# Attention normalisation moved from the output tiles to the queries, value sums folded into the output weights, in a hand-set order

## The chip, the cores and the metric

The kernel runs on one core of one Trainium2 chip. The metric is the device time of one launch in microseconds (us). Single runs of one kernel mostly agree within 0.3%; the 2% that counts as a clear difference is 11.5 us here. In profile lines, PE is TensorE (matmul), DVE is VectorE, ACT is ScalarE, SP is SyncE; "SPq" is the queue from which SyncE issues transfers.

## The reference

A layer with linear attention is followed by a token-mixing MLP.

```python
h  = x + A(layernorm(x))                   # S = 2048 tokens, D = 1024, 32 heads of 32
h2 = h + B(layernorm(h))                   # B mixes tokens: S -> 3584 -> S

def A(x):                                  # cut
    q, k, v = split(x @ wqkv)
    phi = lambda t: where(t > 0, t + 1, exp(t)) + 1e-6
    pq, pk = phi(q), phi(k)
    kv = einsum("bhsd,bhse->bhde", pk, v); z = einsum("bhsd->bhd", pk)
    num = einsum("bhqd,bhde->bhqe", pq, kv)
    den = einsum("bhqd,bhd->bhq", pq, z)[..., None] + 1e-6
    return merge_heads(num / den) @ wo
```

Per head, the output row is `(pq @ kv / den) @ wo`. The reciprocal of `den` is one number per token and head, so it may be applied to `pq` instead; and `kv @ wo` does not depend on the token, so it can be computed once. That algebra is the change.

## The kernel before

The MLP's matmuls are Strassen-like: seven products instead of eight, and in the groups called quads the first and fifth product are split once more into 256-wide matmuls. PSUM is the memory that TensorE adds into; to evacuate a tile is to copy it out of there, to seed it is to copy the residual in first. The stretch that matters starts when keys and values are summed. What remains are 22 units of the query projection (eight 128x512 matmuls each), then 16 output tiles of 128 tokens (sixteen matmuls each), then the first mixer product. Cut:

```python
a3w = actx.enter_context(tc.tile_pool(name="a3w", bufs=3))       # h_bf: evacuated output tiles
xrpool = actx.enter_context(tc.tile_pool(name="xrpool", bufs=XRL + 1))   # residual tiles, 4 buffers

def attn_num_den(i):                          # one tile of 128 tokens
    for j in range(ND):                       # 8 matmuls of 132 columns: 128 numerators, 4 denominators
        b, sl = divmod(j, JPB)
        nc.tensor.matmul(nd_ps[:, b, sl * NCOL:(sl + 1) * NCOL],
                         lhsT=pqT[:, j, i * P:(i + 1) * P], rhs=ndrhs[:, j, :], start=True, stop=True)
    # ... ScalarE: reciprocal as exp(-ln(den)); VectorE: three scalings from PSUM into o_sb
    return o_sb

def attn_transpose(i, o_sb):                  # by DMA, back into the place of the queries
    nc.sync.dma_start_transpose(out=pqT[:, :, i * P:(i + 1) * P], in_=o_sb[:])

def out_proj(i):
    xr = xrs.pop(i)
    h_bf = a3w.tile([P, D], BF16, name="h_bf")
    for dc in range(NDC):
        ap_ = acc_tile()                      # one of five PSUM accumulators, in turn
        nc.scalar.copy(ap_[:, 0:CW], xr[:, dc * CW:(dc + 1) * CW])      # seed with the residual
        # ... eight matmuls pqT x wo_sb on top of the seed
        nc.scalar.copy(h_bf[:, dc * CW:(dc + 1) * CW], ap_[:, 0:CW])
        nc.vector.bn_stats(st[:, dc, :], ap_[:, 0:CW])
    # ... mean, variance, scale
    nc.sync.dma_start(h_dram[i][:], h_bf[:])  # needed again for the last addition

for i in range(NS):
    if i % 2 == 0 and i // 2 < TPC:
        attn(NS - TPC + i // 2)
    if i + XRL < NS:
        load_xr(i + XRL)                      # one residual tile ahead per output tile
    out_proj(i)
    if i >= 2:
        normalize_h(i - 2)
```

A scheduler may reorder what is not pinned. In the timelines ScalarE and SyncE's transfer queue work through their instructions in the order of the built program.

Of the kernel before, what the change touches and what calls it, by code (L numbers as in the profile page):

```python
# [1 line left out]

# [19 lines left out]
XRL = 3  # L22
ACT_SET_LN_EXP = 6
# [4 lines left out]
def kernel(  # L28
# [28 lines left out]
    NCOL = P + HB  # L57
    JPB = BANK // NCOL
    NNB = (ND + JPB - 1) // JPB
# [40 lines left out]
    for q in range(HB):  # L100
        nc.vector.memset(maskbd[q * DH:(q + 1) * DH, q * DH:(q + 1) * DH], 1.0)
        nc.vector.memset(m4[q * DH:(q + 1) * DH, q:q + 1], 1.0)
# [5 lines left out]
    nc.vector.memset(eps_den[:], DEN_EPS)  # L108
# [27 lines left out]
    def load_w1(u, half):  # L136
        if half == 0:
            w1_tiles[u] = w_tile(wpool, WLEN)[:, 0:NS * CW].rearrange("p (k f) -> p k f", f=CW)
        k = slice(half * NSP, (half + 1) * NSP)
        nc.sync.dma_start(  # L140
            w1_tiles[u][:, k, :],
            B_w1[:, u * CW:(u + 1) * CW].rearrange("(k p) f -> p k f", p=P)[:, k, :],
        )
# [8 lines left out]
    def combine(e, o, t2, t3, t4):  # L152
        lo, hi = slice(0, CW), slice(CW, 2 * CW)
        sub = ALU.subtract
        nc.vector.tensor_tensor(t3, o[:, hi], e[:, hi], sub)
        nc.vector.tensor_tensor(e[:, hi], e[:, hi], e[:, lo], sub)
        nc.vector.tensor_tensor(t2, o[:, hi], e[:, hi], sub)
        if t4 is not None:
            nc.vector.tensor_tensor(t4, o[:, lo], t2, sub)
# [29 lines left out]
    def inner_moving(M, nk, pool, name):  # L189
# [4 lines left out]
        def sums():  # L194
            for o, a, b in ((t3, b22, b12), (b12, b12, b11), (t2, b22, b12), (t4, b21, t2)):
                nc.vector.tensor_tensor(o, a, b, ALU.subtract)
# [3 lines left out]
    class Held:  # L200
        on = False

        def __init__(self, engine):
            self.engine = engine

        def __getattr__(self, name):
            op = getattr(self.engine, name)
            return (lambda *a, **kw: pin(op(*a, **kw))) if Held.on else op  # L208

    dve, pe = Held(nc.vector), Held(nc.tensor)  # L210

# [55 lines left out]
    class Product7:  # L267
# [61 lines left out]
        def p6(self, ks=None):  # L329
            self.mm(6, self.B, False, ks)  # L330
            if self.whole(ks):
                self.C = psy.tile([P, BANK], F32, tag="y", name="psC1")
                nc.scalar.copy(self.C[:], self.B[:])  # L333
# [18 lines left out]
        def p4(self, ks=None):  # L352
            for a, b, ps in self.parts:
                self.mm(4, ps, False, ks, cols=slice(a, b))
                if self.whole(ks):
                    self.evac(1, 0, ps, a, b)
            if self.whole(ks):
                self.done()

    class Mixer1(Product7):  # L360
# [11 lines left out]
        def evac_shared(self, fh, ps):  # L372
            t = pools["t"].tile([P, BANK], F32, tag=f"t{fh}", name="t1")
            nc.vector.tensor_tensor(t[:], ps[:], self.e[:], ALU.add)
            self.evac(fh, 1, t)

        def done(self):
            e = gE[:, self.p, :]
            nc.vector.tensor_tensor(e[:, CW:D], e[:, CW:D], e[:, 0:CW], ALU.subtract)
# [39 lines left out]
    class Quad:  # L419
        def __init__(self, sts, mov1, mov5):  # L420
            self.sts = sts
            self.mov1, self.mov5 = mov1, mov5

# [29 lines left out]
        def interleave(self, n, fs):  # L453
            steps = [(f, k) for f in fs for k in range(self.sts[0].nk)]
            t = len(steps)
            cuts = [0, (5 * t + 8) // 16, (9 * t + 8) // 16, (12 * t + 8) // 16, t]

            def fill(q):
                part = steps[cuts[q]:cuts[q + 1]]
                for f in fs:  # L460
                    ks = [k for g, k in part if g is f]
                    if ks:
                        f(ks)

            for f in (n.i1, 0, n.i6, n.i2, 1, n.i5, n.i7, 2, n.i3, 3, n.i4):
                fill(f) if isinstance(f, int) else f()

# [46 lines left out]

        def run(self, pend, nxt, on_p4=nop, before_p7=nop, on_p7=nop, cut=None):
            interleave = self.interleave
            if self.mov1 is not None:
                for st in self.sts:
                    st.begin()
                interleave(self.in1, [st.p4 for st in pend])  # L520
# [9 lines left out]
            interleave(self.in5, [st.p6 for st in self.sts])  # L530
            pre = nxt.pre if nxt is not None else (lambda m: None)
# [8 lines left out]
            pre(7)  # L540
            for st in self.sts:
                st.p3()
            pre(3)
# [14 lines left out]
    def run_pair(st, pend, nxt, after1=nop, after5=nop, on_p4=nop, before_p7=nop, on_p7=nop):  # L558
        st.p1()
        after1()  # L560
        if not pend:
            h = st.nk // 2
            st.p5(list(range(st.nk - 1)))
            st.p2(list(range(h)))
            st.p5([st.nk - 1])
        else:
            for q in pend:
                q.p4()
            on_p4()
            st.p5()  # L570
        after5()
        nxt.pre(5)
        st.p6()
        nxt.pre(6)
        st.p2(None if pend else list(range(h, st.nk)))
        before_p7()
        st.p7()
        on_p7()
        nxt.pre(7)
        st.p3()  # L580
        nxt.pre(3)
        return [st]

    with ExitStack() as actx:
        a3s = actx.enter_context(tc.tile_pool(name="a3s", bufs=4))
        a3w = actx.enter_context(tc.tile_pool(name="a3w", bufs=3))
        a3o = actx.enter_context(tc.tile_pool(name="a3o", bufs=3))
# [7 lines left out]
        ndrhs = pqpool.tile([P, ND, NCOL], BF16)  # L595
# [10 lines left out]
        with ExitStack() as a1:  # L606
# [476 lines left out]
            for n in range(3):  # L1083
                q_fill()
            for b in range(NKB):
                j0, n = b * KPB, min(KPB, ND - b * KPB)
                nc.vector.tensor_tensor(
                    ndrhs[:, j0:j0 + n, 0:P],
# [5 lines left out]
                    ndrhs[:, j0:j0 + n, P:NCOL],  # L1094
# [6 lines left out]
        warmctx.close()  # L1101
        wpool = sactx.enter_context(tc.tile_pool(name="wpool", bufs=2, side="right"))
# [4 lines left out]

        a3p = actx.enter_context(ExitStack())
        ndp = a3p.enter_context(tc.tile_pool(name="ndp", bufs=1, space=PSUM))
        nd_ps = ndp.tile([P, NNB, BANK], F32, name="nd_ps")  # L1110
        nc.vector.memset(nd_ps[:], 0.0)

        with ExitStack() as a3:

            def attn_num_den(i):
                for j in range(ND):
                    b, sl = divmod(j, JPB)
                    nc.tensor.matmul(
                        nd_ps[:, b, sl * NCOL:(sl + 1) * NCOL],
                        lhsT=pqT[:, j, i * P:(i + 1) * P],  # L1120
                        rhs=ndrhs[:, j, :],
                        start=True,
                        stop=True,
                    )
                dn = a3s.tile([P, NNB * JPB * HB], F32, name="dn")
                nc.scalar.activation(
                    dn[:].rearrange("p (b s c) -> p b s c", b=NNB, c=HB),
                    nd_ps[:, :, 0:JPB * NCOL].rearrange("p b (s c) -> p b s c", c=NCOL)[:, :, :, P:NCOL],
                    ACT.Ln,
                    bias=eps_den[:],  # L1130
                    scale=1.0,
                )
                rd = a3s.tile([P, NNB * JPB * HB], F32, name="rd")
                nc.scalar.activation(rd[:], dn[:], ACT.Exp, scale=-1.0)
                o_sb = a3o.tile([P, D], BF16, name="o_sb")
                for b in range(NNB):
                    nsl = min(JPB, ND - b * JPB)
                    blk = nd_ps[:, b, 0:nsl * NCOL].rearrange("p (s c) -> p s c", c=NCOL)
                    nc.vector.tensor_tensor(
                        o_sb[:, b * JPB * P:(b * JPB + nsl) * P].rearrange("p (s h e) -> p s h e", h=HB, e=DH),  # L1140
                        blk[:, :, 0:P].rearrange("p s (h e) -> p s h e", e=DH),
                        rd[:, b * JPB * HB:(b * JPB + nsl) * HB].rearrange("p (s h) -> p s h", h=HB).unsqueeze(3).to_broadcast([P, nsl, HB, DH]),
                        ALU.mult,
                    )
                return o_sb

            def attn_transpose(i, o_sb):
                nc.sync.dma_start_transpose(out=pqT[:, :, i * P:(i + 1) * P], in_=o_sb[:])

            xrs = {}  # L1150

            def load_xr(i):
                xr = xrpool.tile([P, D], BF16, name="xr")
                nc.sync.dma_start(xr[:], x[i * P:(i + 1) * P, :])
                xrs[i] = xr

            def out_proj(i):
                xr = xrs.pop(i)
# [3 lines left out]
                for dc in range(NDC):  # L1162
                    ap_ = acc_tile()
                    if SEED_RESIDUAL:
                        nc.scalar.copy(ap_[:, 0:CW], xr[:, dc * CW:(dc + 1) * CW])
                    for j in range(ND):
                        nc.tensor.matmul(  # L1167
                            ap_[:, 0:CW],
                            lhsT=pqT[:, j, i * P:(i + 1) * P],
                            rhs=wo_sb[:, j, dc * CW:(dc + 1) * CW],  # L1170
                            start=(j == 0 and not SEED_RESIDUAL),
                            stop=(j == ND - 1 and SEED_RESIDUAL),
                            skip_group_check=SEED_RESIDUAL,
                        )
                    if not SEED_RESIDUAL:
                        nc.tensor.matmul(ap_[:, 0:CW], lhsT=ident[:], rhs=xr[:, dc * CW:(dc + 1) * CW], start=False, stop=True)
                    nc.scalar.copy(h_bf[:, dc * CW:(dc + 1) * CW], ap_[:, 0:CW])  # L1177
                    nc.vector.bn_stats(st[:, dc, :], ap_[:, 0:CW])  # L1178
# [215 lines left out]
```

## Time and profile before

| | before |
|---|---|
| time, median | 573.18 us |
| span of the profiled execution | 571.5 us |
| TensorE / VectorE / ScalarE busy | 563.7 / 390.2 / 272.0 us |
| granted TensorE clock, mean | 0.999 |

From the page of the kernel before: busy time by engine, TensorE's busy share in 40 slices (tenths), and the chain of work that ended last by engine.

```profile
...
PE 563.7 (99%) x3124; PEld 293.3 (51%) x3124; DVE 390.2 (68%) x759; ACT 272.0 (48%) x585; POOL 1.8 (0%) x8
...
PE   7999999999999999999999999999999999999997
...
PE 95%; DVE 3%; ACT 1%; issue 1%; DMA 1%; ACTq 0%
...
```

TensorE is busy all the time between start-up and tail, and the chain is TensorE too. So a microsecond counts only if TensorE works less or waits less. From the chain of waits in order of time (start, length, what):

```profile
...
135.18 3.45 PE acc_t L1019 x16
...
139.10 3.45 PE acc_t L1019 x16
...
```

Sixteen 512-wide matmuls take 3.45 us, 216 ns each. The next sixteen start 3.92 us after the first, so the block of eight 132-wide matmuls between them costs 0.47 us. From the waits view, TensorE's only idle time outside start-up (us in total, times, longest):

```profile
...
PE psA L297 <- ACT psB L316: 0.7, 1, 0.7
...
PE psA L297 <- DVE hE L1189: 0.2, 1, 0.2
```

Both belong to the step from the output projection to the mixer. TensorE's timeline there (start, length, instructions, in brackets the idle time before):

```profile
...
231.74 3.83 PE L1167 MATMUL acc_t<-wo_sb,pqT 128*128 128x512 bf16 x17
235.50 1.68 PE L297 MATMUL psA<-hE,wq 128*128 128x512 f16 x7
...
239.96 1.02 PE L297 MATMUL psA<-hO,wq 128*128 128x512 f16 x4 [0.74 <-ACT psB L316]
...
```

The chain has every quad of the first MLP half at 23.57 us.

### The profile page before, as it was taken

The numbers are of one execution on the slowest core, as the hardware profiler recorded it, in microseconds if no ns is written. First come the engines' busy times: TensorE is split into PE (matmuls) and PEld (weight loads), VectorE is DVE, ScalarE is ACT, GpSimd is POOL, SyncE is SP. The second block draws the span as 40 slices with busy tenths as digits, with TensorE's granted clock in tenths as the row PEclk, the third lists the DMA queues.
The fourth block names the chain that finished last, engine by engine and source line by source line (L and its number), as shares of the span: only waits on it lengthen the run. The fifth ranks groups of instructions, "written<-read, shape, count | busy, mean of one in ns | idle before, by whom it ended". The sixth has DMA issues, their size and how long they took to land.

```text
span 571.5 us, 8308 instructions
## 1 busy us (share of the span) xinstructions
PE 563.7 (99%) x3124; PEld 293.3 (51%) x3124; DVE 390.2 (68%) x759; ACT 272.0 (48%) x585; POOL 1.8 (0%) x8
## 2 busy tenths in 40 slices
PE   7999999999999999999999999999999999999997
PEld 3444444455554444346555565555445655645643
DVE  6898887546767879873735627453979749659625
ACT  4747777666667776445445354453220411311211
POOL 1000000000000000000000000000000000000000
PEclk9999999999999999999999999999999999999999
DMA  9933432029536753104041340413892932912111
GB/s 303 357 76 79 89 74 38 19 96 323 118 72 127 177 178 111 55 2 147 1 148 28 120 148 1 148 48 81 205 255 84 244 96 75 278 56 73 38 47 46
DMA packets 97800, 66.61 MB, mean 117 GB/s; under 512 B 32082, under 2 KB 91744, under 8 KB 97760
## 3 DMA queue, kind: packets, MB, share of 16 engines
q1 hardware_dynamic: 97024, 65.42, 41.7%
q10 hardware_dynamic: 672, 0.66, 0.3%
q8 instruction: 24, 0.39, 0.3%
q14 instruction: 16, 0.13, 0.1%
q0 software_dynamic: 64, 0.01, 0.0%
HBM read 50.34 MB, written 8.39 MB: 103 GB/s over the span
## 4 chain that ended last, share of the span: by engine, by line
PE 95%; DVE 3%; ACT 1%; issue 1%; DMA 1%; ACTq 0%
PE psB L297 10%; PE psC L297 10%; PE acc_t L1019 9%; PE acc_t L1167 9%; PE psC L208 7%; PE psA L297 7%; PE psI L230 7%; PE psB L208 6%; PE psI L208 6%; PE psB L750 4%; PE psC L750 4%; PE psA L750 4%; PE psA L208 3%; PE acc_t L674 2%; PE psE L750 2%; PE psE L297 1%
## 5 line engine op out<-in xcount | busy, mean ns | idle before, releaser
L297 PEld LDWEIGHTS <-sa 128*128 128x128 f16 x436 | 42.6, 98 | 46.8 <-issue 0.7
L1019 PE MATMUL acc_t<-xnT,wq_sb 128*128 128x512 bf16 x256 | 58.0, 379 | 0.0
L1167 PE MATMUL acc_t<-wo_sb,pqT 128*128 128x512 bf16 x256 | 56.1, 379 | 0.0
L208 PEld LDWEIGHTS <-wq 128*128 128x128 bf16 (+1 forms) x357 | 34.5, 98 | 31.3
L297 PEld LDWEIGHTS <-wq 128*128 128x128 bf16 (+1 forms) x324 | 31.6, 98 | 33.1 <-issue 1.0
L208 PE MATMUL psC<-gs,wq 128*128 128x512 f16 (+2 forms) x210 | 45.0, 365 | 0.0
L1167 PEld LDWEIGHTS <-pqT 128*128 128x128 bf16 x256 | 24.8, 98 | 29.0
L1019 PEld LDWEIGHTS <-wq_sb 128*128 128x128 bf16 x256 | 24.5, 98 | 27.4
L166 ACT ACTIVATE e_sb<-acc_t 128x512 bf16<-128x512 f32 x40 | 23.9, 597 | 26.5 <-PE acc_t L1019 24.3
L170 DVE TENSOR_SCALAR e_sb<-e_sb 128x512 bf16<-128x512 bf16 x64 | 18.5, 289 | 25.4 <-ACT e_sb L166 24.8
L208 PEld LDWEIGHTS <-sa 128*128 128x128 f16 x231 | 22.6, 98 | 18.6
L750 PEld LDWEIGHTS <-xs 128*128 128x128 f16 x208 | 20.0, 98 | 23.3 <-DVE xs L736 1.3
L208 DVE TENSOR_TENSOR ot<-ot,hr 128x512 bf16<-128x512 bf16 (+2 forms) x27 | 11.2, 415 | 28.1 <-ACT ot L406 27.7
L333 ACT COPY psC<-psB 128x512 f32<-128x512 f32 x22 | 12.5, 570 | 35.1 <-PE psB L297 21.5
L297 PE MATMUL psB<-hT,sa 128*128 128x512 f16 x112 | 28.4, 379 | 0.0
L441 DVE TENSOR_TENSOR e<-psI,es 128x256 f32<-128x256 f32 x12 | 5.1, 425 | 34.0 <-PE psI L230 34.0
L297 PE MATMUL psC<-hT,wq 128*128 128x512 f16 x112 | 28.3, 379 | 0.0
L750 PE MATMUL psA<-wkv,xnT 128*128 128x512 bf16 x104 | 26.7, 379 | 0.0
L1178 DVE BATCH_NORM_STATS2 hst<-acc_t 128x6 f32<-128x512 f32 x32 | 22.1, 692 | 6.7 <-ACT h_bf L1177 6.5
L297 PE MATMUL psA<-hO,wq 128*128 128x512 f16 x112 | 25.6, 379 | 0.7 <-ACT psB L316 0.7
L297 PE MATMUL psB<-hO,sa 128*128 128x512 f16 x112 | 25.5, 379 | 0.0
L297 PE MATMUL psC<-hT,sa 128*128 128x512 f16 x112 | 25.5, 379 | 0.0
(184 smaller groups left out, 1022.9 us busy)
## 6 DMA issues: line engine op xcount, KB each, us to landing
wq<-in_B_w_dram SPq DMA_DIRECT2D x14, 1024.0 KB, 7.7
wq<-in_B_w_dram SPq DMA_DIRECT2D x8, 1792.0 KB, 9.1
xr<-in_A_x_dram SPq DMA_DIRECT2D x16, 256.0 KB, 3.1
h_dram<-h_bf SPq DMA_DIRECT2D x16, 256.0 KB, 2.2
hr<-h_dram SPq DMA_DIRECT2D x32, 128.0 KB, 2.4
out_dram<-ot SPq DMA_DIRECT2D x31, 128.0 KB, 1.8
x_sb<-in_A_x_dram SPq DMA_DIRECT2D x15, 256.0 KB, 3.2
wkv<-in_A_wqkv_dram SPq DMA_DIRECT2D x2, 1024.0 KB, 9.0
```

The source lines that it names most:

```text
L166: pin(nc.scalar.activation(e_sb[:], src, ACT.Exp))
L170: pin(nc.vector.tensor_scalar(e_sb[:], e_sb[:], 1.0, PHI_EPS, ALU.min, ALU.add))
L208: return (lambda *a, **kw: pin(op(*a, **kw))) if Held.on else op
L230: pe.matmul(ps, lhsT=self.lhs[m][:, k, :], rhs=self.mov[m][:, k, :], start=(start and k == 0), stop=(k == self.nk - 1), skip_group_check=True,
L297: pe.matmul(ps[:, cols], lhsT=lhs[:, k, :], rhs=mv(k)[:, cols], start=(start and k == 0), stop=(k == self.nk - 1), skip_group_check=True,)
L333: nc.scalar.copy(self.C[:], self.B[:])
L441: dve.tensor_tensor(self.sts[m].e[:, self.cols(h)], ps, es, ALU.add)
L674: mm = nc.tensor.matmul(pp[:, 0:CW], lhsT=xnT[:, kt, i * P:(i + 1) * P], rhs=wkv[:, kt, c * CW:(c + 1) * CW], start=(kt == 0), stop=(kt == ...
L750: pin(nc.tensor.matmul(ps[:], lhsT=lhs[:, k, :], rhs=rhs[:, k, :], start=(start and k == 0), stop=(k == hk2 - 1), skip_group_check=True,))
L1019: nc.tensor.matmul(qp[:, 0:SW], lhsT=wq_sb[:, kt, j * P:(j + 1) * P], rhs=xnT[:, kt, u * SW:(u + 1) * SW], start=(kt == 0), stop=(kt == ND ...
L1167: nc.tensor.matmul(ap_[:, 0:CW], lhsT=pqT[:, j, i * P:(i + 1) * P], rhs=wo_sb[:, j, dc * CW:(dc + 1) * CW], start=(j == 0 and not SEED_RES ...
L1178: nc.vector.bn_stats(st[:, dc, :], ap_[:, 0:CW])
```

## The change

The intent is to drop the numerator matmuls, their scalings and the DMA transposes of 16 tiles. The `kv` sums are transposed once and folded into the output weights; the denominators are computed for 512 tokens at once; the reciprocals go through DRAM, are broadcast to the partitions of their heads, and scale the queries in place. The order of the engines is set by hand. The first two mixer pairs become a quad whose fifth product is split; in the later quads some sums and evacuations also move (not shown). Residual tiles 4 to 11 get a pool of their own in the space of the layer input and query weights, dead by then. The core of the diff, with cuts:

```diff
-            def attn_num_den(i): ...         # and attn_transpose
+            def fold(j):
+                for c in range(NDC):
+                    cols = slice(c * CW, (c + 1) * CW)
+                    ps = acc_tile()
+                    ht.matmul(ps[:, 0:CW], lhsT=kvT[:, j, :], rhs=wo_sb[:, j, cols], start=True, stop=True)
+                    (hs.copy if c == 0 else hv.tensor_copy)(wf[:, j, cols], ps[:, 0:CW])
+            def den_mm(u):                   # 512 tokens
+                ps = ndp.tile([P, SW], F32, tag="den", name="den_ps")
+                for o in range(2):
+                    for g in range(4):
+                        j = 4 * o + g
+                        ht.matmul(ps[g * QR:(g + 1) * QR, :], lhsT=zz[:, j, (1 - o) * HB:(1 - o) * HB + QR],
+                                  rhs=pqT[:, j, u * SW:(u + 1) * SW], start=(o == 0), stop=(o == 1),
+                                  skip_group_check=True, tile_position=(0, g * QR))
+                return ps
+            def den_inv(u, ps):
+                # ... rd = exp(-ln(den))
+                hd.dma_start(rd_dram[u][:], rd[:])
+                # ... 8 broadcasts of 128 KB: hd.dma_start(rdb[...], rows[h, q]....to_broadcast([DH, 4, SW]))
+            def scale_q(u, h):
+                v = pqT[:, h * NH:(h + 1) * NH, u * SW:(u + 1) * SW]
+                hv.tensor_tensor(v, v, rdbs.pop((u, h))[:], ALU.mult)
...
+            a3w = a3.enter_context(tc.tile_pool(name="a3w", bufs=3))
+            xr2pool = a3.enter_context(tc.tile_pool(name="xr2pool", bufs=XR2))      # XR2 = 8
...
             for i in range(NS):
-                out_proj(i)
+                seed(i + 1)
+                out_mm(i)
+                if i == 0:
+                    for k in range(XRL + 1, XRL + 4):
+                        load_xr(k)
+                    den(NSC - 1)                             # last block: write, then 8 broadcasts
+                    for k in range(XRL + 4, XRL + XR2 + 1):
+                        load_xr(k)
+                if i < NS - XRL - XR2 - 1:
+                    load_xr(i + XRL + XR2 + 1)
+                # ... for the last tile, scales and normalisations
+                out_evac(i)                                  # h_bf, statistics, write to h_dram
```

In this diff `ht`, `hv`, `hs` and `hd` are TensorE, VectorE, ScalarE and SyncE with every instruction pinned in program order.

## The prediction

> **What bounds the kernel.** TensorE. The page's busy table has PE at 563.7 of 571.5 us (99%), VectorE 68%, ScalarE 48%; the chain of waits is 95% PE. In that chain eight 512-wide matmuls take 1.73 us (216 ns each), eight 256-wide ones 0.87 us (109 ns), a block of eight 128x132 numerator/denominator matmuls 0.47 us. So only PE work and PE stalls count. Outside start-up and tail (3.5 and 3.2 us), the waits view shows PE idle for only 0.9 us, at the step from the output projection to the first mixer. Hidden stalls add to it: from 235.5 to 271.5 us the matmuls need 33.7 us (128 at 216 ns, 56 at 109 ns) but take 36.0, so 2.3 us are lost there; each later mixer-1 quad loses 0.2 us (23.57 us for 23.37 us of matmuls).
>
> **Removed on PE.** 16 numerator/denominator blocks: 16 x 0.47 = 7.5 us. The first two fifth products become one inner product: 16 x 216 ns = 3.45 us becomes 28 x 109 ns = 3.05 us, 0.4 us less.
>
> **Added on PE.** 16 fold matmuls: 3.45 us. Eight 128-wide transposes: 0.47 us (129-wide matmuls run at 59 ns). Four denominator blocks of eight 32x512 matmuls. One after the other these would be 4 x 1.73 = 6.9 us, and the change would cost 3 us of PE time. They go to four column tiles of the array; the Trainium skill, "TensorE: Matmul & The Clock Gate", Part 3, has such matmuls run concurrently (2.38x for three tiles); "TensorEngine Tiling", Key Properties, adds that a change of tiling mode drains the array. No tiled matmul is in this trace. My estimate: two passes of 216 ns plus 0.2 to 0.3 us of draining and weight loads, 0.7 us a block, 2.8 us in all. Net PE work: -7.5 - 0.4 + 3.45 + 0.47 + 2.8, about -1.2 us.
>
> **Moved off the path.** VectorE loses 48 numerator scalings from PSUM (16.4 + 6.6 us) and gains eight 128x2048 scalings (1.2 us each, as the 128x2048 subtractions), eight fold copies, a few sums. The 16 output transposes by DMA go. Reciprocals now return through DRAM as 8 broadcasts of 128 KB per block, needed 11 us or more later; such loads land in 2.2 to 3.2 us. I expect little PE waiting: in the fold stretch ScalarE needs 1.8 and VectorE 1.4 us per 2.16 us of PE; in the projection about 2.9 us each per 3.45.
>
> **Stalls.** The hand-set order normalizes tiles 13 and 14 before evacuating 15, then runs both first and both second products (6.9 us) while tile 15 is finished (about 3 us). This should remove about 1.9 of the 2.3 us, some 0.3 us in the projection, some 0.3 us of the quads' losses. New stalls: 0.4 us.
>
> **Sum.** -1.2 - 2.5 + 0.4 = about -3.3 us: 569.9 us, and 8 times in 10 between 567.2 and 573.2. Faster by over 2%: 3%; within 2%: 96%; slower by over 2%: 1%.
>
> **What would show it.** Right: no 128x132 group; each denominator block takes 0.5 to 0.9 us of the PE timeline; fold and transposes 3.9 us; PE idle at the step under 0.4 us. Wrong: denominator blocks of 1.7 us (column tiles ran serially: about 574 us); PE waiting for VectorE's scaling behind a broadcast; PE waiting on seeded accumulators because residual loads or the in-order ScalarE queue came late; the first quad's sums not ready.

## More of the kernel before

SyncE's queue issues, in turn, one transpose, one residual tile and one write of an output tile; this is its timeline at the first write:

```profile
...
181.31 1.23 SPq L1148 DMA_TRANSPOSE pqT<-o_sb  x1
182.63 0.53 SPq L1154 DMA_DIRECT2D xr<-in_A_x_dram  x1
183.25 0.40 SPq L1183 DMA_DIRECT2D h_dram<-h_bf  x1
...
```

## The result, and the profile after

| | before | changed |
|---|---|---|
| time, median | 573.18 us | 580.79 us (579.79 to 581.51, 4 runs) |
| span of the profiled execution | 571.5 us | 579.1 us |
| TensorE busy | 563.7 us (99%) | 563.6 us (97%) |
| granted TensorE clock, mean | 0.999 | 0.994 |

The ratio is 1.0123 (95% interval 1.0097 to 1.0149). A ratio here is the mean time of one kernel's fast runs over that of the other's of the same rounds, so not quite the ratio of the medians in the table. The change costs about 7.6 us; it was forecast to gain 3.3. That is less than the 2%, but the interval leaves out 1.

From the page of the changed kernel, the same lines as before, and the granted clock in tenths per slice:

```profile
...
PE 563.6 (97%) x3049; PEld 289.9 (50%) x3064; DVE 387.9 (67%) x734; ACT 274.4 (47%) x573; POOL 1.8 (0%) x8
...
PE   8999999999999599999999999999999999999997
...
PEclk9999999999999989999999999999999999999999
...
PE 88%; DVE 5%; DMA 4%; ACT 2%; issue 1%; SPq 0%; ACTq 0%
...
```

The slices show where: the fourteenth, from about 188 to 203 us, has TensorE only half busy, and the slice after it a reduced clock. The waits view has one long wait that the kernel before did not have:

```profile
...
PE acc_t L209 <- ACT acc_t L209: 7.5, 1, 7.5
...
```

TensorE's timeline of the stretch:

```profile
...
134.64 0.61 PE L209 MATMUL den_ps<-pqT,zz 128*32 128x512 bf16 x8
135.19 1.90 PE L209 MATMUL acc_t<-xnT,wq_sb 128*128 128x512 bf16 x8
...
182.03 0.62 PE L209 MATMUL den_ps<-pqT,zz 128*32 128x512 bf16 x8
182.58 13.99 PE L209 MATMUL acc_t<-wo_sb,pqT 128*128 128x512 f16 x64
204.06 39.93 PE L209 MATMUL acc_t<-wo_sb,pqT 128*128 128x512 f16 x176 [7.49 <-ACT acc_t L209]
243.83 3.88 PE L209 MATMUL psA<-hE,wq 128*128 128x512 f16 x16
248.10 3.61 PE L209 MATMUL psA<-hO,wq 128*128 128x512 f16 x16 [0.39 <-ACT psB L318]
...
```

Read it in three steps. First, the denominator blocks take 0.55 us each (134.64 to 135.19, 182.03 to 182.58). Second, after four more output tiles TensorE stands still until 204.06. Third, the last projection matmul is over at 243.83, where it was 235.50 before. The clock of that stretch comes from the windows view (stretch; its length; busy us of PE, PE weight load, DVE, ACT, POOL; then the granted clock, the DMA share and GB/s):

```profile
...
200.00:204.00 4.00, 0.00 (x0) 0.00 (x0) 1.32 (x3) 1.94 (x6) 0.00 (x0) 0.61 0.99 382
204.00:206.00 2.00, 1.94 (x5) 0.69 (x5) 1.87 (x5) 1.82 (x6) 0.00 (x0) 0.50 0.38 144
206.00:208.00 2.00, 2.00 (x6) 0.69 (x5) 1.96 (x5) 1.25 (x3) 0.00 (x0) 0.57 0.34 131
208.00:210.00 2.00, 2.00 (x11) 0.94 (x10) 1.56 (x2) 0.36 (x1) 0.00 (x0) 1.00 0.00 0
...
```

After the standstill the clock is at half for nearly four microseconds. The chain has the 144 matmuls from 204.06 on at 33.04 us instead of 144 x 215.8 ns = 31.08 us. Of these 1.96 us, 0.16 are the tail of the last matmul's record (0.38 us long, at a spacing of 0.216 us), so the slow clock costs about 1.8 us; from start to start, too, the 176 matmuls take 39.77 instead of 37.98 us. The standstill with both its ends and the slow clock make 7.49 + 1.96 = 9.45 us. This is what the Trainium skill describes in "TensorE: Matmul & The Clock Gate", Part 1: after an idle window of about 3.4 us the clock falls to half, and about as much sustained work brings it back. In this trace narrow windows put the fall at 200.88, 4.3 us after the last matmul ended (196.57), and the return at 207.70, 3.6 us after work began again; this agrees.

Where the difference of 7.6 us arises can be read by milestones of TensorE's timeline (differences of start times; the last column is an experiment told below):

| stretch (us) | before | changed | e7 |
|---|---|---|---|
| start of the first denominator block to end of projection | 100.95 | 109.19 | 99.75 |
| to the second products of the next quad | 35.87 | 34.46 | 34.60 |
| the next two quads | 47.14 | 47.69 | 47.35 |

The first row alone loses 8.24 us. Without 7.49 + 1.96 us it would have gained 1.2 us. The chain of waits says what happened in it:

```profile
...
182.65 7.03 PE acc_t L209 x32
...
189.70 0.59 ACT h_bf L209
...
190.32 0.71 DVE hst L209
...
191.73 4.89 DMA rdb<-rd_dram
...
196.68 5.24 DMA h_dram<-h_bf
...
202.03 0.59 ACT h_bf L209
...
202.64 1.31 DVE hst L209 x2
...
204.06 2.29 PE acc_t L209 x5
```

Backwards from the end (tiles are counted from 0): tile 5's matmuls (204.06) needed an accumulator that is evacuated and seeded in ScalarE's order; ScalarE was held at the evacuation of tile 3 (202.03), because with three `h_bf` buffers it needs the one of tile 0, which was still being written out (196.68 to 201.92); and that write was issued so late because SyncE's queue had it behind the broadcasts of the last denominator block and six residual loads. The queue's timeline shows the order:

```profile
...
184.10 0.33 SPq L209 DMA_DIRECT2D rd_dram<-rd  x1
188.99 3.65 SPq L209 DMA_DIRECT2D rdb<-rd_dram  x8
192.69 2.81 SPq L209 DMA_DIRECT2D xr<-in_A_x_dram  x6
196.68 0.33 SPq L209 DMA_DIRECT2D h_dram<-h_bf  x1
...
```

Tile 0 was evacuated at 185.0 us, but its write left at 196.68. Of these 11.7 us, SyncE spent 4.0 on the wait for the reciprocals' write to land (4.5 us in all by its waits view), 3.65 on issuing the broadcasts, 2.81 on issuing the loads, and most of the rest, 1.2 us, on a wait that the chain puts down to the landing of a broadcast. The write of tile 0 then took 5.24 us to land, where the median of the 16 such writes is 2.0 us. In the kernel before, the write of tile 0 left at 183.25, between a load and a transpose, right after ScalarE's last copy of the tile (182.59 to 183.17).

### The profile page after: what moved, and what is told of

Read it like the earlier page. It is cut to its first block, busy times and chain, and to the rows that moved or that the text cites. A ratio compares the mean times of both kernels' runs of the same rounds, so it can differ in the third digit from the quotient of the medians.

```text
span 579.1 us, 8134 instructions
## 1 busy us (share of the span) xinstructions
PE 563.6 (97%) x3049; PEld 289.9 (50%) x3064; DVE 387.9 (67%) x734; ACT 274.4 (47%) x573; POOL 1.8 (0%) x8
## 4 chain that ended last, share of the span: by engine, by line
PE 88%; DVE 5%; DMA 4%; ACT 2%; issue 1%; SPq 0%; ACTq 0%
PE acc_t L209 15%; PE psC L209 14%; PE psB L209 13%; PE psI L209 12%; PE psA L209 7%; PE psB L797 4%; PE psC L797 4%; PE psA L797 4%; PE acc_t L721 2%; PE psB L299 2%; PE psA L299 2%; PE acc_t L1066 2%; PE psE L797 2%; PE psC L299 2%; DMA wq<-in_B_w_dram 2%; PE kvps L750 1%
## 5 line engine op out<-in xcount | busy, mean ns | idle before, releaser
L209 PEld LDWEIGHTS <-wq 128*128 128x128 bf16 (+1 forms) x653 | 63.4, 98 | 55.5 <-issue 1.1
L209 PEld LDWEIGHTS <-sa 128*128 128x128 f16 x651 | 63.6, 98 | 54.8
L209 PE MATMUL acc_t<-wo_sb,pqT 128*128 128x512 f16 x256 | 57.5, 387 | 7.5 <-ACT acc_t L209 7.5
L209 PEld LDWEIGHTS <-is 128*128 128x128 f16 x376 | 36.7, 98 | 18.3 <-issue 3.5
L209 PE MATMUL acc_t<-xnT,wq_sb 128*128 128x512 bf16 x188 | 43.1, 379 | 0.2
L209 DVE BATCH_NORM_STATS2 hst<-acc_t 128x6 f32<-128x512 f32 x32 | 20.9, 689 | 18.4 <-ACT h_bf L209 18.2
L209 PEld LDWEIGHTS <-wq_sb 128*128 128x128 bf16 x192 | 18.5, 98 | 23.0 <-issue 1.3
L209 DVE TENSOR_TENSOR e<-psI,es 128x256 f32<-128x256 f32 x20 | 8.5, 424 | 31.9 <-ACT es L255 19.3
L209 ACT CAST h_bf<-acc_t 128x512 bf16<-128x512 f32 x32 | 17.7, 587 | 19.4 <-DMA h_dram<-h_bf 10.3
L209 DVE TENSOR_TENSOR psA<-psI,es 128x256 f32<-128x256 f32 x18 | 7.8, 433 | 26.4 <-PE psI L209 23.8
```

The source lines that it names most:

```text
L209: return (lambda *a, **kw: pin(op(*a, **kw))) if self.always or Held.on else op
```

## The experiments

The changed kernel was not run again beside the experiments. The kernel before was: its median is 573.14 to 573.33 us in all their rounds (573.18 above), so medians of different rounds are compared here.

**Theory A:** the in-order queue is the cause. The write of tile 0 stands behind one write, eight broadcasts and six residual loads; three `h_bf` buffers pass the delay on to ScalarE, and ScalarE's own order passes it on to TensorE. **Theory B:** the residual loads or broadcasts come late themselves, and the wait on the write is incidental. **Theory C:** the DMA engines are simply full there (in the windows view their share is 1.01 between 196 and 200 us), so the write would be slow wherever it stood.

### e1 and e5: more buffers

```diff
-            a3w = a3.enter_context(tc.tile_pool(name="a3w", bufs=3))
+            a3w = a3.enter_context(tc.tile_pool(name="a3w", bufs=5))
```

> The changed kernel with 5 instead of 3 buffers for the evacuated output tiles, nothing else. Theory A (the write of output tile 0 stands in the in-order SyncE queue behind the last denominator block's nine transfers and six residual loads; with 3 buffers ScalarE cannot evacuate tile 3 until that write has landed at 201.9 us, and PE stands still for 7.5 us): two more buffers buy two tiles of 3.45 us, so the stall shrinks from 7.5 to about 0.6 us, the clock stays at full speed (another 1.9 us back), and the time falls from 580.8 to about 572.0 us. Theory B (the residual loads or the broadcasts themselves come late, the wait of ScalarE on the write is incidental): PE still waits 4 us or more, for the seeds or for VectorE's scaling, and the time stays above 576.

This one did not build: the file had six buffers, and with the pool of eight residual tiles six do not fit. It was mended to five and run again with a new expectation.

> The run that did not build, with 5 buffers for the evacuated output tiles instead of 3 (they fit), all else as in the changed kernel. ScalarE's write queue trick of the last round is not in it. If the three buffers are what passes the late write on to PE, two more buy two tiles of 3.45 us: PE waits at most 0.6 us there, the clock stays full, 571.5 to 572.3 us. If the seeds or the broadcasts come late by themselves, PE waits 3 us or more and the time is above 575.

Measured: 572.35 us (571.75 to 573.81), ratio 0.9987 (0.9973 to 1.0000), clock 1.000. In the waits view of this run:

```profile
...
PE acc_t L209 <- ACT acc_t L209: 0.8, 1, 0.8
...
```

The expected 0.6 us is 0.8, and the median lies just above the expected 571.5 to 572.3 us. The profile is of the fastest of the four runs (571.75 us); the slowest (573.81 us) had a clock of 0.996, so its wait may have been longer, which no trace shows. Two buffers bought 7.49 - 0.82 = 6.7 us of waiting, and two tiles are 2 x 3.45 = 6.9 us. Theory B had 3 us or more. The waiting was for a buffer.

### e2: the later residual loads, after the writes

```diff
-                    for k in range(XRL + 4, XRL + XR2 + 1):
-                        load_xr(k)
-                if i < NS - XRL - XR2 - 1:
-                    load_xr(i + XRL + XR2 + 1)
...
                 out_evac(i)
+                load_xr(i + XRL + 4)
```

> The changed kernel with residual tiles 7 to 15 issued one at a time, each after the write of an output tile, instead of five at once ahead of the first write. Own pool and 3 buffers kept. Theory A: the write of tile 0 now stands only behind the broadcasts, leaves at about 193 instead of 196.7 us, lands at 195 to 197 instead of 201.9; PE still waits 1 to 3 us; time 573 to 576 us. Theory B (residual loads late): loads come later still, so no gain or a loss: 580 us or more.

Measured: 575.89 us (574.72 to 576.55), ratio 1.0050 (1.0033 to 1.0067), clock 0.999. The write left at 192.49 instead of 196.68. In the waits view:

```profile
...
PE acc_t L209 <- ACT acc_t L209: 2.7, 3, 1.9
...
```

Later loads made it faster by 4.9 us, which theory B excludes. The longest wait, 1.9 us, did not lower the clock: the mean between 198.5 and 202.5 us is 1.00.

### e3: the writes on another queue

```diff
-                hd.dma_start(h_dram[i][:], h_bf[:])
+                hs.dma_start(h_dram[i][:], h_bf[:])
```

> The changed kernel with the 16 writes of output tiles issued from ScalarE's own queue, so that they don't stand behind the transfers of the SyncE queue; same bytes at the same time. Theory A: the write of tile 0 leaves at about 185 us and lands before 191; no PE stall, full clock; time about 571.4 us, at most 1 us more for ScalarE's issuing. Theory C (the DMA engines are simply full between 185 and 200 us: 2 MB of weights, 1 MB of broadcasts, 2.3 MB of residual tiles): the write is slow wherever it is issued, and at least half of the stall of 7.5 us stays; time above 575.

Measured: 571.66 us (570.91 to 572.87), ratio 0.9974 (0.9959 to 0.9989), clock 1.000. TensorE's timeline has no gap left in the projection:

```profile
...
182.48 52.27 PE L209 MATMUL acc_t<-wo_sb,pqT 128*128 128x512 f16 x240
234.59 3.87 PE L209 MATMUL psA<-hE,wq 128*128 128x512 f16 x16
...
```

The timelines of ScalarE and SyncE have the write of tile 0 and, after it, the write of the reciprocals:

```profile
...
184.97 0.34 ACTq L209 DMA_DIRECT2D h_dram<-h_bf  x1
...
```

```profile
...
189.47 0.33 SPq L209 DMA_DIRECT2D rd_dram<-rd  x1
...
```

The edit changes only the queue, and all bytes are the same, so theory C as it was put falls: it left at least half of the stall. But the bytes do not move at the same time: SyncE issued the write of the reciprocals at 189.47 instead of 184.10, after a wait that the profile puts down to the landing of an output tile's write, and the broadcasts from 191.21 on instead of 188.99. And a weaker form of theory C stays open. In the changed kernel the late write took 5.24 us, some 3 us above the median of 2.0; that part of the stall may well be the load on the DMA engines, and no run separates it. Here the Trainium skill needs a reader's care. "DMA: Bandwidth & Descriptors", Issuing engines are not separate DMA queues, says that starting transfers from several engines only saves the sequencer's time to start them. In bandwidth that may be so. But where one in-order queue holds a short urgent write behind transfers that wait for something else, this run shows a gain of 9.1 us from a second queue.

### e4: less traffic, same order

```diff
-                if n in (4, 5, 18, 19):
-                    load_w1(n // 18, n % 2, pin)
+                if n in (4, 5):
+                    load_w1(0, n % 2, pin)
...
                 out_evac(i)
+                if i in (6, 7):
+                    load_w1(1, i % 2, pin)
```

> The changed kernel with the two 1 MB loads of the second mixer weight tile moved from the last query units to output tiles 6 and 7. Queue order of the writes unchanged. Theory A: the reciprocals' write and broadcasts get through about 3 us sooner (the write took 4.5 us beside the weight load), the rest of the queue stands as before: stall 3 to 5 us instead of 7.5; time 575 to 577. Theory C (bandwidth): with 2 of some 5 MB out of the way the stall goes almost wholly, below 1 us; time about 571.5.

Measured: 579.27 us (578.74 to 580.87), ratio 1.0110 (1.0094 to 1.0125), clock 0.994. The waits view and two windows (columns as above):

```profile
...
PE acc_t L209 <- ACT acc_t L209: 4.9, 1, 4.9
...
```

```profile
...
201.40:203.00 1.60, 1.60 (x4) 0.54 (x4) 1.50 (x5) 1.45 (x4) 0.00 (x0) 0.50 0.45 174
203.00:205.00 2.00, 2.00 (x6) 0.73 (x5) 1.94 (x4) 1.55 (x5) 0.00 (x0) 0.50 0.34 131
...
```

The wait of 4.9 us is inside theory A's 3 to 5 us and far from theory C's "below 1 us". The time was outside the expected 575 to 577 us, though: the expectation had forgotten that a wait of 4.9 us still halves the clock. Here this even costs more than in the changed kernel: from start to start the 176 matmuls from 201.40 on take 40.36 instead of 37.98 us, 2.4 us more. In both traces the clock stays at half for 6.8 us, but here it fell already 2.9 us after the last matmul ended (196.53 to 199.42), so less of the 6.8 us lay in the wait.

### e9: order alone

The edit on top of e2: the last block's transfers go after the write of tile 0.

```diff
-                    den(NSC - 1)
+                    rd_last = den_inv(NSC - 1, den_mm(NSC - 1))
...
                 out_evac(i)
+                if i == 0:
+                    den_send(NSC - 1, rd_last)               # the write to DRAM and 8 broadcasts
                 load_xr(i + XRL + 4)
```

> Order alone: three buffers, all writes on the SyncE queue, later residual loads as in the second experiment, and the last denominator block's nine transfers issued after the write of output tile 0 instead of ahead of it. If the place of that one write in the queue is what costs, it leaves at about 185 us and tile 3 finds its buffer; the next write stands behind the broadcasts, leaves at about 193 and lands at 196 to 197, when tile 4 needs it at 196.6: PE waits 0 to 1 us, time 571.5 to 572.7 us. If order is not enough with three buffers: PE waits 1.5 us or more, 573 us or above.

Measured: 574.90 us (574.12 to 576.30), ratio 1.0037 (1.0020 to 1.0054), clock 1.000. That is 1.0 us better than e2, on which it builds. The waits view has 2.0 us of TensorE waiting, and the chain of waits shows why:

```profile
...
193.14 0.59 ACT h_bf L209
...
193.93 5.32 DMA h_dram<-h_bf
...
199.35 0.59 ACT h_bf L209
...
```

The write of tile 0 left at 185.05, as wanted. Now tile 1's write stands behind the broadcasts, leaves at 193.93 and takes 5.32 us; ScalarE waits for its buffer one tile later. The hope that order would do with three buffers is refuted. The jam moved on by one tile.

### e6 and e7: a version that beats both, with and without the pool

e6 is e2 and e5 together. e7 undoes the second part of the change: no pool for residual tiles 4 to 11, four shared buffers as in the kernel before, and six `h_bf` buffers in the room.

```diff
-                    pool = xr2pool if XRL < i <= XRL + XR2 else xrpool
-                    xr = pool.tile([P, D], BF16, name="xr")
+                    xr = xrpool.tile([P, D], BF16, name="xr")
...
-            a3w = a3.enter_context(tc.tile_pool(name="a3w", bufs=3))
-            xr2pool = a3.enter_context(tc.tile_pool(name="xr2pool", bufs=XR2))
+            a3w = a3.enter_context(tc.tile_pool(name="a3w", bufs=6))
...
-                    for k in range(XRL + 1, XRL + 4):
+                    for k in range(XRL + 1, XRL + 3):
                         load_xr(k)
                     den(NSC - 1)
-                    # ... the loads of tiles 7 to 11, and of 12 on
...
                 out_evac(i)
+                load_xr(i + XRL + 3)
```

> Five buffers and the residual loads each after a write, writes still on the SyncE queue: the write of tile 0 leaves at about 192.5 us and lands at 196.3, while the sixth tile needs its buffer only at about 200 us. No PE wait in the projection: 571.2 to 571.7 us, as with the writes on ScalarE's queue or up to 0.4 us better, since ScalarE no longer spends time on issuing.

> The second part of the change undone: no own pool for residual tiles 4 to 11, four shared buffers as before, tiles 4 and 5 loaded ahead of the last denominator block, each later one after a write and six tiles ahead; the room goes to six buffers for the evacuated tiles. If the pool of eight is not needed once the queue is unblocked: no PE wait in the projection, 571.2 to 571.7 us. If the loads need the lead that the pool gives them: PE waits for a seed, 1 us or more, 572.5 us or above.

Measured: e6 571.42 us (571.31 to 571.76), ratio 0.9967 (0.9955 to 0.9980); e7 571.30 us (571.23 to 571.90), ratio 0.9967 (0.9953 to 0.9981). Their rounds have the kernel before at 573.33 us. SyncE's and TensorE's timelines of e7:

```profile
...
188.23 3.65 SPq L209 DMA_DIRECT2D rdb<-rd_dram  x8
191.99 0.36 SPq L209 DMA_DIRECT2D h_dram<-h_bf  x1
...
```

```profile
...
182.24 51.97 PE L209 MATMUL acc_t<-wo_sb,pqT 128*128 128x512 f16 x240
234.05 3.87 PE L209 MATMUL psA<-hE,wq 128*128 128x512 f16 x16
...
```

In e7 the first write still leaves late, at 191.99 us, behind the same broadcasts. With six buffers nobody needs it sooner, and the 240 matmuls run in one piece. The pool of eight residual tiles is not needed: e6 and e7 do not differ. Its room can go to buffers for what has to be written; whether the sixth of them gains anything was not tested.

### e8: does the denominators' order matter?

```diff
-                for o in range(2):
-                    for g in range(4):
+                for g in range(4):
+                    for o in range(2):
```

(on top of e3)

> Writes on ScalarE's queue, and the eight matmuls of a denominator block issued column group by column group (both matmuls of one group in succession) instead of all four groups alternating. If the four groups run side by side only because neighbours go to different column tiles, a block takes 1.0 to 1.8 us instead of 0.55, and 2 to 5 us are lost over four blocks. If the order does not matter, the block stays at 0.55 us.

Measured: a single look, 571.55 us, state unknown. TensorE's timeline:

```profile
...
181.98 0.62 PE L209 MATMUL den_ps<-pqT,zz 128*32 128x512 bf16 x8
182.54 52.26 PE L209 MATMUL acc_t<-wo_sb,pqT 128*128 128x512 f16 x240
...
```

From 181.98 to 182.54 the block takes 0.56 us, as before. So in this run the column tiles run side by side even when neighbours in the program go to the same tile.

## Why the prediction was wrong, and where it was right

1. **What bounds the kernel: right.** TensorE does; e7 gains only what TensorE saves in work and waits (the table's three stretches make -2.3 us, the medians -2.0).
2. **TensorE's work: right in the mechanism and nearly in size.** It put each denominator block at 0.7 us and got 0.55 (four blocks: 2.2 instead of 2.8 us). Leaving out the 0.4 us of the split product, its terms make -7.5 + 3.45 + 0.47 + 2.8 = -0.8 us for the first stretch. With the measured blocks it would be -1.4; the table has -1.2 us in e7. The feared case, column tiles one after the other at 1.7 us, did not come.
3. **"New stalls: 0.4 us": this is the step that failed.** It measured 7.49 us of waiting plus about 1.8 us of slow clock. The prediction weighed broadcasts by when VectorE needs them ("needed 11 us or more later") and found them in time, which they were. It never asked what stands behind them in the same in-order queue; and where it had such transfers land in 2.2 to 3.2 us, the broadcasts took 3.7 us (median of 32, page of the changed kernel) and the last block's write ahead of them 4.8. It listed late residual loads and "the in-order ScalarE queue" among the things that would make it wrong, but costed neither, and the write of an output tile was not on the list. ScalarE's queue was indeed the last link, but VectorE's scaling behind a broadcast and late residual loads were not the cause. e3, e5, e6 and e7, which change the write's queue or its buffers, take away all or nearly all of the wait; e2, e4 and e9, which change order or traffic only, leave 2.7, 4.9 and 2.0 us of it.
4. **A stall's second cost was missing.** The clock was not in the prediction. In the profiled executions, waits of 0.8 and 1.9 us (e5, e2) left it at full speed; waits of 4.9 and 7.5 us (e4, changed) halved it, for 6.8 us both times.
5. **The step to the mixer: over-rated.** Forecast were -1.9 us of stalls and -0.4 us of work. Measured are -1.4 us in the changed kernel and -1.3 in e7 (second row of the table). A wait of 0.39 us on the same kind of ScalarE copy stays, where 0.74 us was.
6. **The quads: wrong in sign.** Forecast were -0.3 us. The two quads in the third row take 0.55 us more in the changed kernel and 0.21 in e7; the later ones keep their 23.57 us in the changed kernel. In the changed kernel's chain, the next weight tile's loads (9.38 us until they land) come just before that. That this causes the loss was not tested and stays open.

With the failed term mended, the forecast of 569.9 us meets 571.3 us of e7. The rest of 1.4 us is mainly points 5 and 6.

## What to carry to other kernels

When a change adds transfers, write down for each queue the order in which they will be issued, and ask of every later transfer which buffer it sets free and who waits for that buffer; that a new transfer arrives in time for its own reader is only half the check. Where an urgent write must follow slow transfers, give it more buffers (one buffer bought about one tile of time here) or another queue, before trying to perfect the order. And cost a long TensorE wait with the slow clock that follows: here it added a quarter to a wait of 7.5 us and half to one of 4.9, and nothing to one of 1.9.

## What the Trainium skill lacked or had wrong

- "DMA: Bandwidth & Descriptors", Issuing engines are not separate DMA queues: it lacks the head of the line. A second issuing queue is said to save only the time to start a transfer, which is usually small. Moving 16 writes of 256 KB to ScalarE's queue brought 580.8 to 571.7 us, because they no longer stood behind the transfers in SyncE's queue (e3). In the changed kernel the first write had stood there for 11.7 us: about 6.5 while 14 transfers were started, and most of the rest while SyncE waited for others to land.
- "TensorE: Matmul & The Clock Gate", Part 3: it has 2.38x for three column tiles and none for four. Here a block of eight 32x512 matmuls on four column tiles, change of mode included, takes 0.55 us against 8 x 216 ns = 1.73 us one after the other, 3.1x. The order within the block made no difference (0.56 us, e8); the page does not say that it need not alternate.
- "TensorEngine Tiling", Key Properties: it names a drain at a change of tiling mode without a size. Two passes of 216 ns are 0.43 us, so drains and weight loads of a block cost about 0.12 us here, an estimate.
- "TensorE: Matmul & The Clock Gate", Part 1: it has the clock fall after at least one idle window of about 3.4 us. In e4 it fell 2.9 us after the last matmul's end (which the profile models), so a somewhat shorter wait was enough there. Otherwise the runs agree: no lower clock after waits up to 1.9 us.
